# A new written order for the attention and Mish feed-forward kernel: first batch, weight steps and repeating part each at new places

## The chip, the cores and the metric

The kernel runs as one program on one core of a Trainium2 chip. The metric is the device time of one execution in microseconds (us), as the median of three runs. The engines are named as in the profile: PE is TensorE, DVE is VectorE, ACT is ScalarE, POOL is GpSimd and SP is SyncE, which issues most of the transfers.

## What is computed

Cut to what matters (B = 4 batches, H = 8 heads, S = 768 positions, D = 64; d_model = 512, d_ff = 2048):

```
q_assign = argmax(q_n @ c_n.T);  k_assign = argmax(k_n @ c_n.T)   # 16 clusters per head
scores = where(q_assign == k_assign, q @ k.T / 8, -1e9)
attn = softmax(scores) @ v
x = attn with its heads side by side                               # 3072 x 512
h = x @ w_in                                                       # 512 -> 2048
out = (h * tanh(softplus(h))) @ w_out                              # 2048 -> 512
```

## The kernel before

The attention is cut into 32 heads (`n`) of three units each, 96 units (`i`), 24 to a batch. A unit is 256 queries of one head, in two halves (`a`) of 128. One half goes through `scores` (L630 and L635: four matmuls into one of two PSUM buffers of the tag S), `rowmax` (L647, DVE), `expo` (L659, ACT, output `p`), the sum's reciprocal, and a transposition of `p`. In batch 0 PE transposes `p` in f32 (`p_lo`, L707) and DVE and ACT copy the result out of PSUM (L726, L728); in the later batches POOL and DVE split `p` into two f16 parts (`hl`, L697 and L714), and SP transposes these by DMA (L730). `pv` (L750) multiplies by the values for two units at a time into one buffer `o`; in batch 0 a few matmuls more (L762) bring the reciprocals into `o`, and `rb` (L794), `xf` (L795) and two more steps make `x` from it. The two S buffers are shared with the cluster products: `assign_mm` (L542, tile `as`) and `assign_put` (L588, tile `put`) each take one in turn, once for four heads; DVE reads `put` into `stg` (L609), and DMAs carry rows of `stg` into the operands `Z` and `T` of a head (L620, L621). `prep_hi`, `prep_lo` and the four copies make the operands A, B, T and Z of a head, partly on POOL (L483, L486, L499), partly by DMA (L513).

The weights are loaded in 32 steps (`stage`, L240 and L246), rebuilt as f32 (`w_low` L267 on POOL, `w_abs` L258 on ACT, `w_f32` L275 on DVE), squared on PE (`gram`, L295), and scaled into f16 pairs (`w_hi` L333, `w_lo` L346). All of this stands between the units of batch 0.

From unit 24 on the feed-forward network runs beside the attention of the next batch: `m1` (L827 to L829, 12 matmuls of half a tile `h`), `e_mish` (L836), `e_gh` (L840, POOL), `e_gl` (L848, DVE) and `m2` (L864 to L866, six matmuls for each of eight steps `f` of an output tile `O`), then `m_out` (L872). Two `m1` tiles and four `m2` steps go with two units.

No scheduler decides the order. Each operation is entered with a time by `Plan.at`; `Plan.run` sorts them by that number, `after` pulls forward what an operation needs, and `tie` binds the instructions of each engine to that order. The times come from the tables `T` (mostly batch 0) and `N` (the repeating part and, in the lists `u`, `w` and `ws`, one number for each unit and weight step). The numbers are places in a sort, not measured times.

Of the kernel before, what the change touches and what calls it, by code (L numbers as in the profile page):

```python
# [26 lines left out]
class Plan:  # L27
# [9 lines left out]
        self.state = {}  # L37

    def at(self, t, fn, *args):
        self.ops[fn.__name__, *args] = (t, len(self.ops), fn, args)  # L40

    def issue(self, op):
        if op not in self.state:
# [28 lines left out]
def tile_clustered_attention_mish_ffn(  # L72
# [1200 lines left out]
    ('vh', 0): 5,  # L1273
    ('vh', 1): 45,
    'vh_step': 1,
    'v_sqd': -1.793,
    'cent_put': -17.25,
    'ffn': 23.993,
    'w_f': 0.331,
    'w_q': 0.827,  # L1280
    'w_lo': 0.305,
    ('z', 'prep_hi'): -17.4,
    ('z', 'prep_lo'): -15.2,
    ('z', 'copy_t'): -17.3,
    ('z', 'copy_a'): -15.0,
    ('z', 'copy_b'): -15.01,
    ('z', 'copy_z'): -15.1,
    ('z', 'assign_mm'): -15.0,
    ('z', 'assign_turn'): -15.05,
    ('z', 'assign_max'): -14.9,  # L1290
    ('z', 'assign_hot'): -14.8,
    ('z', 'assign_back'): -14.7,
    ('z', 'assign_put'): -14.6,
    ('z', 'hot_direct'): -14.55,
    ('z', 'assign_stg'): -14.4,
    ('z1', 'prep_hi'): -16.637,
    ('z1', 'copy_t'): 0.652,
    ('z1', 'prep_lo'): -0.394,
    ('z1', 'copy_z'): 0.103,
    ('z1', 'copy_b'): 0.753,  # L1300
    ('z1', 'copy_a'): 0.423,
    'as_turn': 1.351,
    'as_max': -0.357,
    'as_hot': 4.283,
    'as_back': 0.815,
    'as_put': 1.374,
    'as_stg': 1.508,
    'n_late': 9,
    'wide': 24,
    'v_s0': 36.614,  # L1310
    'act_q': 3,
    'xbufs': (5, 7, 4),
    'v_sq': 20.406,
    'assign': -1.297,
    'hot_copy': -0.251,
    'copy_a': -0.21,
    'copy_b': -0.38,
    'copy_z': -0.725,
    'copy_t': -0.806,
    'prep_lo': 1.071,  # L1320
    'prep_hi': 3.185,
    'load': -3.206,
    'raw': 4,
    ('f_ws', 0): 0,
    ('f_ws', 1): 1,
# [22 lines left out]
    ('f_b', 1): 1,  # L1348
    ('f_l', 0): 0.096,
    ('f_l', 1): 1,  # L1350
    ('w_l', 0): 2.19,
    ('w_l', 1): 1.226,
    'v0': -19.148,
    'v_d': -1.18,
    ('q_hi', 0): 2.631,
    ('q_lo', 0): 0.521,
    ('q_trans', 0): 0.78,
    ('q_hi', 1): 0.793,
    ('q_lo', 1): 3.324,
    ('q_trans', 1): 1.225,  # L1360
    ('f_w', 0): 1,
    ('f_w', 1): 0.659,
    'units0': 24,
# [5 lines left out]
    'O': 1,  # L1369
    ('ws1', 0): 2.668,  # L1370
    ('ws1', 1): -3.407,
    ('scores', 0): -0.068,
    ('rowmax', 0): -0.01,
    ('expo', 0): 0.345,
    ('recip', 0): 2.622,
    ('scores', 1): 0.349,
    ('rowmax', 1): 0.599,
    ('expo', 1): 6.966,
    ('recip', 1): 1.335,
    'pv': 1.42,  # L1380
    'pv_step': 0.487,
    'v_scale': 0.114,
    'pv_out': 2.609,
    ('w_s', 0): -0.341,
    ('w_s', 1): -0.361,
    ('f_sh', 0): 0.995,
    ('f_sh', 1): 1,
}


N = {
    ('load', 0): -7.458,
    ('load', 1): -10.096,
    ('load', 2): -6.974,
    ('load', 3): -4.979,
    'prep_hi': -3.418,
    'prep_lo': 0.494,
    'copy_t': -2.17,
    'copy_z': -2.427,
    'copy_a': -1.038,  # L1400
    'hot_copy': -2.049,
    'copy_b': -1.075,
    'assign_mm': -4.285,
    'assign_turn': -1.043,
    'assign_max': -4.058,
    'assign_hot': 0.071,
    'assign_back': -3.503,
    'assign_put': -0.183,
    'assign_stg': -2.372,
    'v_load': 16.573,  # L1410
    'v_sq': 18.112,
    'v_scale': 21.77,
    'v_max': 22.2,
    'v_pair': 10,
    'v_high': 26.705,
    'v_low': 27.262,
    'v_d': 2.046,
    'E': [0.355, 0.767, 1.154, 1.513],
    'scores': 2.166,
    'rowmax': -0.272,  # L1420
    'expo': -0.103,
    'total': 6.164,
    'recip': 0.144,
    'p_hi': 11.217,
    'p_lo': 1.549,
    'ptrans': 0.865,
    'pv': [5.55, 13.269, 7.015],
    'pv_out': 6.881,
    'x_lo': 2.789,
    'm1': [0.368, 0.616, 0.939, 1.346],  # L1430
    'e_mish': [4.782, 1.75],
    'e_gh': [1.685, 3.448],
    'e_gl': [1.743, 2.41],
    'm2': [4.854, 4.854, 4.854, 4.854, 4.854, 4.854, 4.854, 4.854, 4.881, 4.881, 4.881, 4.881, 4.881, 4.881, 4.881, 4.881],
    'm_out': -0.431,
    'm_store': 0.376,
# [3 lines left out]
}  # L1440


# [26 lines left out]
```

## Time and profile before

| | us |
|---|---|
| runs of the kernel before | 907.83, 908.76, 910.40 |
| median | 908.76 |
| profiled execution, first to last instruction (span) | 908.0 |
| PE busy in the span | 850.7 (94%) |
| DVE busy | 701.2 (77%) |
| ACT busy | 516.8 (57%) |
| POOL busy | 416.9 (46%) |

The page names the span of the profiled execution and no other time of it; the span stands between the fastest run and the median, 0.76 us under the median. A row of the timeline gives start, length, engine, line, operation and tiles, and in square brackets how long the engine stood idle just before and what ended that. SPq and ACTq are the moments at which an engine's queue issued a DMA.

### The profile page before, as it was taken

To read this page: it belongs to the slowest core of one execution; us is meant where nothing else is said; L and a number is where in the kernel's file an instruction comes from. 1 tells how busy PE (TensorE), PEld (TensorE's weight loads), DVE (VectorE), ACT (ScalarE), POOL (GpSimd) and SP (SyncE) were. 2 spreads that over 40 slices of the span, in tenths; PEclk is the share of its full clock that TensorE was granted. 3 is DMA by queue.
4 is the path that set the end of the run, shared out by engine and by line. 5 is a ranking of instruction groups with operands and counts; after the bars stand their busy time and mean duration, and the time that the engine had idled before them with its cause. 6 is when DMAs were issued, how large, how long until landed. Compare 5 with 4: busy or idle time off the path is not lost.

```text
span 908.0 us, 17381 instructions
## 1 busy us (share of the span) xinstructions
PE 850.7 (94%) x6671; PEld 611.1 (67%) x6671; DVE 701.2 (77%) x1178; ACT 516.8 (57%) x876; POOL 416.9 (46%) x410
## 2 busy tenths in 40 slices
PE   7899788869999999899999999999999999999998
PEld 3666565656667666677667667667667676677787
DVE  7879978777897769788987689699887776378841
ACT  6767867655556565556565666556556565145520
POOL 1443638565556445456555455466555544110000
PEclk9999999999999999999999999999999999999999
DMA  8645582258677796679779787679587675200001
GB/s 326 209 142 161 161 243 59 48 100 170 127 152 156 145 241 117 116 159 182 142 136 173 186 178 144 121 152 197 113 137 150 140 143 93 48 12 12 2 19 41
DMA packets 253058, 121.49 MB, mean 134 GB/s; under 512 B 230288, under 2 KB 230800, under 8 KB 252976
## 3 DMA queue, kind: packets, MB, share of 16 engines
q1 hardware_dynamic: 247632, 108.46, 54.4%
q10 hardware_dynamic: 5344, 11.93, 6.2%
q8 instruction: 52, 0.85, 0.4%
q14 instruction: 30, 0.25, 0.1%
HBM read 35.72 MB, written 6.29 MB: 46 GB/s over the span
## 4 chain that ended last, share of the span: by engine, by line
PE 48%; DVE 22%; issue 9%; ACT 8%; POOL 7%; DMA 5%; ACTq 0%; SPq 0%; POOLq 0%; DVEq 0%
DVE m L647 6%; PE o L750 6%; PE h L827 5%; DVE hl L714 5%; PE h L828 5%; PE h L829 5%; PE s L630 4%; PE O L864 4%; PE O L866 4%; PE O L865 4%; PE s L635 4%; DVE g L848 4%; ACT p L659 3%; POOL g L840 2%; DMA pt<-hl 2%
## 5 line engine op out<-in xcount | busy, mean ns | idle before, releaser
L659 ACT ACTIVATE p<-s,m 128x768 f32<-128x768 f32 x192 | 173.0, 901 | 116.6 <-DVE l L671 89.9
L697 POOL TENSOR_SCALAR hl<-p,l 128x768 f16<-128x768 f32 x144 | 160.2, 1117 | 123.9 <-DVE l L679 43.3
L647 DVE TENSOR_REDUCE m<-s 128x1 f32<-128x768 f32 x192 | 182.4, 950 | 32.2 <-PE s L635 28.8
L714 DVE SCALAR_TENSOR_TENSOR hl<-p,l,hl 128x768 f16<-128x768 f32 x144 | 181.2, 1259 | 8.6 <-POOL hl L697 8.2
L827 PE MATMUL h<-x,w 128*128 128x256 f16 x640 | 176.9, 276 | 3.8 <-ACT u L836 3.6
L828 PE MATMUL h<-x,w 128*128 128x256 f16 x640 | 175.5, 274 | 0.0
L829 PE MATMUL h<-x,w 128*128 128x256 f16 x640 | 175.5, 274 | 0.0
L630 PE MATMUL s<-A,B 128*128 128x384 f32 x384 | 122.0, 399 | 19.9 <-ACT p L659 14.7
L840 POOL TENSOR_SCALAR g<-u,mscg 128x512 f16<-128x512 f32 x80 | 72.5, 906 | 143.6 <-ACT u L836 135.3
L866 PE MATMUL O<-w,g 128*128 128x512 f16 x320 | 121.4, 379 | 7.6 <-DVE g L848 7.6
L864 PE MATMUL O<-w,g 128*128 128x512 f16 x320 | 121.8, 381 | 2.8 <-POOL g L840 2.7
L865 PE MATMUL O<-w,g 128*128 128x512 f16 x320 | 121.3, 379 | 0.0
L635 PE MATMUL s<-Z,T 80*128 80x384 f32 x384 | 100.1, 342 | 0.7 <-DMA T<-stg 0.6
L827 PEld LDWEIGHTS <-w 128*128 128x128 f16 x768 | 75.5, 98 | 32.5 <-issue 21.8
L630 PEld LDWEIGHTS s<-A,B 128*128 128x128 f32 x384 | 62.9, 191 | 44.0 <-ACT p L659 24.3
L848 DVE SCALAR_TENSOR_TENSOR g<-u,mscg,g 128x512 f16<-128x512 f32 x80 | 83.9, 1049 | 9.2 <-POOL g L840 6.8
L659 ACT ACT_TABLE_LOAD x35 | 44.9, 1283 | 79.3 <-DVE m L647 72.1
L828 PEld LDWEIGHTS <-w 128*128 128x128 f16 x768 | 75.9, 99 | 14.9 <-issue 4.2
L829 PEld LDWEIGHTS <-w 128*128 128x128 f16 x768 | 75.5, 98 | 9.0
L750 PE MATMUL o<-pt,v 128*64 128x256 f16 x1296 | 78.1, 274 | 0.5 <-DVE l L671 0.5
L750 PEld LDWEIGHTS <-v 128*64 128x64 f16 x1296 | 67.7, 110 | 15.7 <-issue 12.4
L635 PEld LDWEIGHTS s<-Z,T 80*128 80x128 f32 x384 | 70.2, 190 | 1.5 <-DMA T<-stg 0.9
(225 smaller groups left out, 1311.5 us busy)
## 6 DMA issues: line engine op xcount, KB each, us to landing
qk<-in_qk_dram SPq DMA_DIRECT2D x32, 384.0 KB, 5.0
stage<-in_w_in_dram SPq DMA_DIRECT2D x16, 512.0 KB, 7.6
stage<-in_w_out_dram SPq DMA_DIRECT2D x16, 512.0 KB, 5.1
vraw<-in_vP_dram SPq DMA_DIRECT2D x16, 384.0 KB, 6.5
T<-A ACTq DMA_DIRECT2D x30, 192.0 KB, 3.2
Z<-B SPq DMA_DIRECT2D x30, 192.0 KB, 3.3
B<-T ACTq DMA_DIRECT2D x28, 192.0 KB, 3.7
out_dram<-osb SPq DMA_DIRECT2D x20, 256.0 KB, 4.4
```

The source lines that it names most:

```text
L630: nc.tensor.matmul(s[:, j, :384], st["B", n][:, q0 : q0 + P], st["A", n][:, j * 384 : (j + 1) * 384], start=True, stop=False,)
L635: nc.tensor.matmul(s[:, j, :384], st["T", n][: D + NCL, q0 : q0 + P], st["Z", n][: D + NCL, j * 384 : (j + 1) * 384], start=False, stop=True,)
L647: nc.vector.tensor_reduce(m, st["s", i, a][:, :, :384], axis=AX.XY, op=ALU.max, negate=True)
L659: nc.scalar.activation(p.rearrange("p (n x) -> p n x", n=2), st["s", i, a][:, :, :384], AF.Exp, bias=st["m", i, a], scale=1.0, accum_out=l,)
L697: nc.gpsimd.tensor_scalar(t[:, 0], p, r, 1.0, op0=ALU.mult, op1=ALU.mult)
L714: nc.vector.scalar_tensor_tensor(t[:, 1], p, r, t[:, 0], op0=ALU.mult, op1=ALU.subtract)
L750: nc.tensor.matmul(o[s * D : s * D + D, :256], v if early else v[:, int(part == 1)], st["pt", 2 * m + s][:, :, c + (0 if early or part < 2 ...
L827: nc.tensor.matmul(o, wh, xh, start=(c == 0), stop=False)
L828: nc.tensor.matmul(o, wh, xl, start=False, stop=False)
L829: nc.tensor.matmul(o, wl, xh, start=False, stop=(c == 3))
L864: nc.tensor.matmul(o, gh, wh, start=(f == 0 and fi == 0), stop=False)
L866: nc.tensor.matmul(o, gl, wh, start=False, stop=(f == 7 and fi == 1))
```

## The change

No instruction is added or taken away, and none goes to another engine: each engine has the same instructions as before, in another order. The numbers of the tables are new for the operands of the first heads, all 24 units of batch 0 (`u`), all 32 weight loads (`w`) and 16 scalings (`ws`), and the repeating part; `m2` has one number for each of its 16 steps where there were two values. `Plan.at` gets a table `SHIFT`, which is empty here.

```diff
     def at(self, t, fn, *args):
-        self.ops[fn.__name__, *args] = (t, len(self.ops), fn, args)
+        op = fn.__name__, *args
+        self.ops[op] = (t + SHIFT.get(op, 0), len(self.ops), fn, args)
...
-    ('z', 'hot_direct'): -14.55,
-    ('z', 'assign_stg'): -14.4,
+    ('z', 'hot_direct'): -7.188,
+    ('z', 'assign_stg'): -13.122,
...
-    'm2': [4.854, 4.854, 4.854, 4.854, 4.854, 4.854, 4.854, 4.854, 4.881, 4.881, 4.881, 4.881, 4.881, 4.881, 4.881, 4.881],
+    'm2': [4.92, 5.951, 7.713, 5.196, 5.86, 5.59, 7.546, 4.752, 4.8, 4.886, 6.84, 4.982, 4.196, 4.758, 9.839, 5.211],
...
+SHIFT = {
+   
+}
```

In the order of the change every line number is one higher than before.

**DVE at the start**, from the first cluster product to the maxima of unit 0 (`m0_0` and `m0_1` belong to its two halves). Before:

```order
L573 STREAM_TRANSPOSE hott0_237<-hot0_235 128x768
L600 TENSOR_SCALAR Z_0_200<-put0_239 16x256
L602 TENSOR_SCALAR T_0_192<-put0_239 16x256
L602 TENSOR_SCALAR T_0_192<-putT_243 16x512
L609 TENSOR_SCALAR stg0_253<-put0_239,put_b_137 128x768
L493 SCALAR_TENSOR_TENSOR B_1_270<-qk1_146,scq_138,A_1_196 128x768
L509 CAST Z_1_272<-B_1_270 64x768
L647 TENSOR_REDUCE m0_0_280<-s0_0_275 128x1
```

And now:

```order
L574 STREAM_TRANSPOSE hott0_237<-hot0_235 128x768
L610 TENSOR_SCALAR stg0_249<-put0_239,put_b_137 128x768
L601 TENSOR_SCALAR Z_0_198<-put0_239 16x256
L603 TENSOR_SCALAR T_0_192<-put0_239 16x256
L603 TENSOR_SCALAR T_0_192<-putT_243 16x512
L494 SCALAR_TENSOR_TENSOR B_1_268<-qk1_146,scq_138,A_1_231 128x768
L648 TENSOR_REDUCE m0_0_281<-s0_0_276 128x1
L280 TENSOR_SCALAR w1_284<-w1_284 128x512
```

`stg0` stands first, and the cast `Z_1` has left the rows ahead of `m0_0`. On ACT two of the squares of the values (`vq0_3`, `vq0_2`) stand ahead of `Z_0` now, and the copy `A_1` behind `p0_0`.

**PE and SP around units 9 to 12.** On PE, the product `put1` and its neighbours, before:

```order
L707 MATMUL q8_1_3_983<-ident_129,p8_1_948 128x128 x3
...
L762 MATMUL o3_908<-ident_129,l7_808 64x128 x2
L630 MATMUL s9_1_1000<-A_3_770,B_3_783 128x384 x2
L635 MATMUL s9_1_1000<-Z_3_785,T_3_773 128x384 x2
L588 LDWEIGHTS put_w_136
L588 MATMUL put1_1007<-hott1_962,put_w_136 128x512
```

And now:

```order
L708 MATMUL q8_1_3_978<-ident_129,p8_1_946 128x128 x3
L589 LDWEIGHTS put_w_136
L589 MATMUL put1_984<-hott1_962,put_w_136 128x512
...
L763 MATMUL o3_923<-ident_129,l7_815 64x128 x2
L631 MATMUL s9_1_1005<-A_3_761,B_3_794 128x384 x2
L636 MATMUL s9_1_1005<-Z_3_796,T_3_764 128x384 x2
```

`put1` has moved ahead of the last third of `pv` and of the score `s9_1`. SP's transfers for the operands of head 4, before:

```order
L513 DMA Z_4_1046<-B_4_1044 64x768
L246 DMA stage20_1093<-in_w_out_dram 128x512
L246 DMA stage21_1115<-in_w_out_dram 128x512
L246 DMA stage22_1137<-in_w_out_dram 128x512
L620 DMA Z_4_1046<-stg1_1035 16x768
L621 DMA T_4_1033<-stg1_1035 16x768
L513 DMA A_4_1030<-A_4_1030 64x768
```

And now:

```order
L514 DMA Z_4_1048<-B_4_1046 64x768
L247 DMA stage19_1055<-in_w_out_dram 128x512
L621 DMA Z_4_1048<-stg1_987 16x768
L622 DMA T_4_1021<-stg1_987 16x768
L247 DMA stage21_1136<-in_w_out_dram 128x512
L514 DMA A_4_1018<-A_4_1018 64x768
L247 DMA stage22_1224<-in_w_out_dram 128x512
```

The copies of head 4 have come forward past `stage22`, and two of them past `stage21`.

**DVE in the repeating part**, at unit 42. Before:

```order
L647 TENSOR_REDUCE m42_0_3930<-s42_0_3925 128x1
L714 SCALAR_TENSOR_TENSOR hl41_1_3957<-p41_1_3854,l41_1_3855,hl41_1_3957 128x768
L848 SCALAR_TENSOR_TENSOR g8_3866<-u17_3910,mscg0_2117,g8_3866 128x512
L647 TENSOR_REDUCE m42_1_3968<-s42_1_3963 128x1
L671 TENSOR_SCALAR l42_0_3936<-l42_0_3936 128x1
```

And now:

```order
L648 TENSOR_REDUCE m42_0_3927<-s42_0_3922 128x1
L715 SCALAR_TENSOR_TENSOR hl41_1_3950<-p41_1_3861,l41_1_3862,hl41_1_3950 128x768
L648 TENSOR_REDUCE m42_1_3961<-s42_1_3956 128x1
L672 TENSOR_SCALAR l42_0_3964<-l42_0_3964 128x1
L680 RECIPROCAL l42_0_3964<-l42_0_3964 128x1
```

The split `g8<-u17` has moved from its place ahead of `m42_1` to one behind `m43_1`. On PE, one `m1` half and one `m2` step stood between `s42_0` and `s42_1`; now three `m2` steps stand there, and the 24 matmuls of `m1` follow `s42_1` in one piece. The same holds at units 34, 50, 58, 66, 74, 82 and 90.

## Rows read from the trace of the kernel before

**Rows 1.** Waits of PE by releaser: us in total, times, longest us
```profile
PE s L630 <- ACT p L659: 14.7, 14, 4.3
PE q L707 <- ACT p L659: 10.2, 8, 2.4
PE O L866 <- DVE g L848: 7.6, 15, 0.9
```

**Rows 2.** Windows: us; busy us (instructions) of PE, PEld, DVE, ACT, POOL; clock; DMA
```profile
0.00:200.00 200.00, 165.50 (x1206) 114.27 (x1207) 162.94 (x298) 138.31 (x263) 96.65 (x116) 0.99 0.55 164
200.00:250.00 50.00, 46.90 (x366) 33.16 (x365) 42.17 (x65) 28.50 (x47) 29.15 (x27) 0.94 0.70 136
250.00:800.00 550.00, 534.09 (x4245) 379.86 (x4245) 433.00 (x710) 308.50 (x504) 287.43 (x263) 1.00 0.73 146
```

**Rows 3.** Timeline of the start: DVE, ACT and PE around the first exponential
```profile
18.84 0.56 DVE L509 CAST Z<-B 64x768 fp32r<-64x768 f32 x1
19.31 0.94 DVE L647 TENSOR_REDUCE m<-s 128x1 f32<-128x768 f32 x1
...
19.96 1.21 ACT L258 ACTIVATE w<-stage 128x512 f32<-128x512 f32 x2
21.20 0.90 ACT L659 ACTIVATE p<-s,m 128x768 f32<-128x768 f32 x1
...
22.25 0.87 PE L707 MATMUL q<-ident,p 128*128 128x128 f32 x6 [2.19 <-ACT p L659]
```

**Rows 4.** Timeline of PE and ACT at unit 5
```profile
52.07 0.41 PE L295 MATMUL gram<-w 128*128 128x128 bf16 x4
...
55.30 0.87 PE L707 MATMUL q<-ident,p 128*128 128x128 f32 x6 [1.46 <-ACT p L659]
...
52.18 0.47 ACT L794 ACTIVATE rb<-o,vsp 128x256 f32<-128x256 f32 x1 [0.56 <-PE o L762]
```

**Rows 5.** Timeline of PE and SP's queue at units 10 and 12
```profile
81.14 0.62 PE L630 MATMUL s<-A,B 128*128 128x384 f32 x2 [1.74 <-DVE stg L609]
...
94.31 0.58 PE L630 MATMUL s<-A,B 128*128 128x384 f32 x2 [2.30 <-DMA A<-A]
...
82.18 4.21 SPq L246 DMA_DIRECT2D stage<-in_w_out_dram  x3
...
87.63 0.77 SPq L513 DMA_DIRECT2D A<-A  x1
```

**Rows 6.** Timeline of PE at units 12 and 13
```profile
102.67 0.55 PE L707 MATMUL q<-ident,p 128*128 128x128 f32 x3 [1.24 <-ACT p L659]
...
106.81 0.44 PE L707 MATMUL q<-ident,p 128*128 128x128 f32 x2 [0.77 <-ACT p L659]
...
109.99 0.40 PE L295 MATMUL gram<-w 128*128 128x128 bf16 x4 [1.61 <-DVE w L275]
```

**Rows 7.** Timeline of PE and ACT at units 16 and 22
```profile
129.69 0.55 PE L707 MATMUL q<-ident,p 128*128 128x128 f32 x3 [2.41 <-ACT p L659]
...
161.44 0.62 PE L630 MATMUL s<-A,B 128*128 128x384 f32 x2 [0.81 <-ACT p L659]
...
128.27 0.48 ACT L728 COPY pt<-q 128x384 f32<-128x384 f32 x1 [3.10 <-DMA Z<-B]
```

**Rows 8.** Timeline of PE at the passage from batch 0 to the repeating part
```profile
190.64 0.27 PE L827 MATMUL h<-x,w 128*128 128x256 f16 x1 [3.00 <-ACT u L836]
...
198.43 0.62 PE L630 MATMUL s<-A,B 128*128 128x384 f32 x2 [4.28 <-ACT p L659]
```

**Rows 9.** Window after the wait at 127.3 us (columns as in rows 2)
```profile
130.70:134.10 3.40, 3.40 (x20) 2.13 (x20) 1.99 (x4) 1.89 (x4) 0.00 (x0) 0.50 0.92 276
```

**Rows 10.** Timeline of the repeating part: one m2 step, and a score's maximum on DVE
```profile
453.42 0.38 PE L864 MATMUL O<-w,g 128*128 128x512 f16 x1
...
454.71 0.49 PE L588 MATMUL put<-hott,put_w 128*128 128x512 bf16 x2
...
458.88 0.52 PE L635 MATMUL s<-Z,T 80*128 80x384 f32 x2
...
462.69 0.96 DVE L647 TENSOR_REDUCE m<-s 128x1 f32<-128x768 f32 x1
```

More of the change, by code (lines that the diff above doesn't have):

```diff
@@ L1275 @@
     'vh_step': 1,
-    'v_sqd': -1.793,
-    'cent_put': -17.25,
+    'v_sqd': -4.857,
+    'cent_put': -17.279,
     'ffn': 23.993,
[L1279 to L1293, printed above, removed]
-    ('z', 'hot_direct'): -14.55,
-    ('z', 'assign_stg'): -14.4,
[L1296 to L1307, printed above, removed]
+    'w_f': 0.342,
+    'w_q': 0.823,
+    'w_lo': 0.291,
+    ('z', 'prep_hi'): -18.102,
+    ('z', 'prep_lo'): -12.511,
+    ('z', 'copy_t'): -17.558,
+    ('z', 'copy_a'): -14.141,
+    ('z', 'copy_b'): -14.199,
+    ('z', 'copy_z'): -16.644,
+    ('z', 'assign_mm'): -11.201,
+    ('z', 'assign_turn'): -12.664,
+    ('z', 'assign_max'): -16.42,
+    ('z', 'assign_hot'): -13.075,
+    ('z', 'assign_back'): -13.196,
+    ('z', 'assign_put'): -12.749,
+    ('z', 'hot_direct'): -7.188,
+    ('z', 'assign_stg'): -13.122,
+    ('z1', 'prep_hi'): -15.657,
+    ('z1', 'copy_t'): -0.271,
+    ('z1', 'prep_lo'): -1.37,
+    ('z1', 'copy_z'): 1.133,
+    ('z1', 'copy_b'): 2.654,
+    ('z1', 'copy_a'): 0.617,
+    'as_turn': 1.904,
+    'as_max': -0.501,
+    'as_hot': 2.44,
+    'as_back': 0.862,
+    'as_put': 0.993,
+    'as_stg': 1.052,
     'n_late': 9,
     'wide': 24,
-    'v_s0': 36.614,
+    'v_s0': 37.618,
     'act_q': 3,
     'xbufs': (5, 7, 4),
[L1313 to L1322, printed above, removed]
+    'v_sq': 20.251,
+    'assign': -1.302,
+    'hot_copy': -0.44,
+    'copy_a': -0.208,
+    'copy_b': -0.408,
+    'copy_z': -0.704,
+    'copy_t': -0.829,
+    'prep_lo': 0.861,
+    'prep_hi': 1.193,
+    'load': -4.609,
     'raw': 4,
@@ L1350 @@
     ('f_l', 1): 1,
[L1351 to L1360, printed above, removed]
+    ('w_l', 0): 1.964,
+    ('w_l', 1): 0.963,
+    'v0': -17.969,
+    'v_d': -4.561,
+    ('q_hi', 0): 2.074,
+    ('q_lo', 0): 0.677,
+    ('q_trans', 0): 0.738,
+    ('q_hi', 1): 0.779,
+    ('q_lo', 1): 4.003,
+    ('q_trans', 1): 1.217,
     ('f_w', 0): 1,
@@ L1371 @@
     ('ws1', 1): -3.407,
[L1372 to L1376, printed above, removed]
+    ('scores', 0): -0.15,
+    ('rowmax', 0): 0.017,
+    ('expo', 0): 0.325,
+    ('recip', 0): 3.718,
+    ('scores', 1): 0.365,
     ('rowmax', 1): 0.599,
-    ('expo', 1): 6.966,
-    ('recip', 1): 1.335,
+    ('expo', 1): 3.444,
+    ('recip', 1): 1.374,
     'pv': 1.42,
-    'pv_step': 0.487,
+    'pv_step': 0.48,
     'v_scale': 0.114,
-    'pv_out': 2.609,
-    ('w_s', 0): -0.341,
-    ('w_s', 1): -0.361,
+    'pv_out': 2.591,
+    ('w_s', 0): 0.201,
+    ('w_s', 1): 0.013,
     ('f_sh', 0): 0.995,
@@ L1391 @@
 N = {
[L1392 to L1411, printed above, removed]
+    ('load', 0): -8.996,
+    ('load', 1): -9.577,
+    ('load', 2): -6.846,
+    ('load', 3): -5.647,
+    'prep_hi': -3.463,
+    'prep_lo': 1.938,
+    'copy_t': -2.608,
+    'copy_z': -2.367,
+    'copy_a': -1.572,
+    'hot_copy': -1.879,
+    'copy_b': -1.003,
+    'assign_mm': -4.289,
+    'assign_turn': -3.32,
+    'assign_max': -4.063,
+    'assign_hot': 1.158,
+    'assign_back': -3.461,
+    'assign_put': 0.705,
+    'assign_stg': -2.445,
+    'v_load': 17.332,
+    'v_sq': 18.055,
     'v_scale': 21.77,
-    'v_max': 22.2,
+    'v_max': 20.003,
     'v_pair': 10,
[L1415 to L1419, printed above, removed]
-    'rowmax': -0.272,
[L1421 to L1433, printed above, removed]
-    'm2': [4.854, 4.854, 4.854, 4.854, 4.854, 4.854, 4.854, 4.854, 4.881, 4.881, 4.881, 4.881, 4.881, 4.881, 4.881, 4.881],
-    'm_out': -0.431,
-    'm_store': 0.376,
[3 rows of a table removed]
+    'v_high': 26.688,
+    'v_low': 27.388,
+    'v_d': 2.039,
+    'E': [0.374, 0.767, 1.238, 1.512],
+    'scores': 1.455,
+    'rowmax': -0.272,
+    'expo': 1.674,
+    'total': 10.193,
+    'recip': 0.131,
+    'p_hi': 11.909,
+    'p_lo': 2.229,
+    'ptrans': 0.846,
+    'pv': [5.141, 16.228, 4.578],
+    'pv_out': 8.203,
+    'x_lo': 2.802,
+    'm1': [0.536, 0.632, 1.227, 1.52],
+    'e_mish': [6.518, 1.693],
+    'e_gh': [1.692, 2.151],
+    'e_gl': [1.771, 3.432],
+    'm2': [4.92, 5.951, 7.713, 5.196, 5.86, 5.59, 7.546, 4.752, 4.8, 4.886, 6.84, 4.982, 4.196, 4.758, 9.839, 5.211],
+    'm_out': -0.434,
+    'm_store': 0.3,
[3 rows of a table added]
+}
+SHIFT = {
 }
```

6 rows, old and new, of the table N are left out of this document.

## The prediction

> **What bounds the kernel now.** I read the busy shares first, then PE's busy time by stretches, then PE's waits by releaser, and last the timeline around each long wait. By stretches [rows 2] PE is the bound of the repeating part: of the 550 us from 250 to 800 it is busy for 534.09, so all that an order could win there is 15.9 us. The first 200 us are different. PE is busy for 165.50 of them and idle for 34.5, while DVE is busy for 162.94: no engine is full, and the end is set by chains that go from one engine to the next. The waits by releaser [rows 1] say which chains: 14.7 us of scores and 10.2 us of transpositions that wait for an exponential on ACT. Only the third, 7.6 us in 15 short waits of the second layer for DVE's `g`, lies in the repeating part. As the change moves instructions and changes none, its effect is the sum of waits that it ends and of waits that it makes.
>
> **The change part by part.** I went through PE's long waits of the first 200 us and asked for each what stands in the new order between its cause and its end.
>
> (a) *Start.* The first transposition waits 2.19 us for the first exponential `p0_0`, which started at 21.20, right behind two weight conversions that ran from 19.96 to 21.17 [rows 3]. Its maximum had been there since 20.25, and 0.56 us of that was the cast `Z_1` ahead of it. Now the squares of the values stand in a gap of ACT before the first cluster product, the copy `A_1` stands behind `p0_0`, and `Z_1` behind `m0_0`. With `stg0` first, the second score no longer waits for its buffer either. I see `p0_0` some 2 us earlier; of that 0.2 is lost again at unit 2. Term: 1.8, bounds 0 and 2.19.
>
> (b) *Unit 5.* Between the end of `rb`'s source (its ACT step starts at 52.18) and the transposition at 55.30 runs a chain rb, xf, x, copy, exponential; PE had one piece of `gram` of 0.41 us to put there, and waited 1.46 [rows 4]. Now four such pieces stand there, three more than before, which covers 1.2 us. Term: 1.1, bounds 0 and 1.46.
>
> (c) *Unit 10.* The score waited 1.74 us until DVE had read `put1` out of one of the two score buffers [rows 5]. `put1` stands now ahead of a third of `pv` and of a whole score, and DVE reads it ahead of `xf` and of a maximum. Term: 1.7, bounds 0 and 1.74.
>
> (d) *Unit 12.* The score waited 2.30 us for the landing of `A<-A`. SP had issued that copy at 87.63, held up by three weight loads, whose issue took from 82.18 to 86.39 since each waits for a stage buffer [rows 5]. Now the copy stands ahead of `stage22`, with only `stage19` and `stage21` between it and `Z_4`, and two stage buffers are freed sooner on DVE. It should be issued some 4 us sooner, more than the wait. Term: 2.3, bounds 0 and 2.30; what it moves back, `stage22`, is a weight step of which no multiplication is near.
>
> (e) *Units 12 and 13.* Three waits, 1.24, 0.77 and 1.61 us [rows 6]. In each, one weight conversion that stood ahead of the awaited operation on ACT or POOL stands behind it now, or the `o` tile that DVE's queue waits for is finished one score earlier. One conversion is 0.6 us [rows 3]. Term: 3 x 0.6 = 1.8, bounds 0 and 3.62.
>
> (f) *Unit 16.* PE waited 2.41 us; ACT had stood for 3.10 us, until `B_6` could be issued after the landing of `Z_6` [rows 7]. The order on ACT is the same there. What changed is what is under way beside `Z_6`: the four value loads stand farther behind it, one weight load is issued after it and no longer before it. The trace has no row for `Z_6` without this company, so the bounds are 0 and 2.41; I take the middle, 1.2, since a reason speaks for each end.
>
> (g) *Unit 22.* 0.81 us behind `put2` [rows 7]; a whole transposition of 0.87 us (length as in rows 3) stands now between the score whose buffer is awaited and the waiting one. Term 0.8.
>
> (h) *Passage.* Waits of 3.00 and 4.28 us [rows 8]. The second ends a chain of mish, POOL's and DVE's split, a maximum, a table load and an exponential; its order on DVE is the same, so that it stays. In the first, PE has 24 matmuls and two scores to place where it had fewer, but the mish comes about 1 us later, behind one more exponential. Term: 0.8, bounds -1 and 3.
>
> The sum is 1.8 + 1.1 + 1.7 + 2.3 + 1.8 + 1.2 + 0.8 + 0.8 = 11.5 us. I count 60% of it, 6.9 us. The reason is the next thing that is late: five of the eight waits are for an exponential, whose maximum stands in DVE's queue, and without 11.5 us of span DVE would be busy for 163 of 188 us, 87%. The repeating part shows DVE at 433.00 of 550, 79%, with PE full [rows 2], so that a part of what PE stops waiting for will be DVE's lateness instead.
>
> In the *repeating part* I cost the change at nothing. The `m2` steps now stand together behind `pv`; that gives DVE's `g` time and takes the same time from the score that follows. At the eight units where `g` moved behind the next maximum the second exponential comes sooner; at two of the cluster products the next score comes closer behind and will wait up to 1 us. Work that hides the rest: PE itself, full for 97% of that stretch. What it costs if that cover goes is the second rival.
>
> The profiled execution has a span of 908.0 us. 908.0 - 6.9 = 901.1, and with the 0.76 us by which the median stands above it, **901.9**.
>
> [...]
>
> **The rivals.** *Given back (0.20).* The eight waits go, and the exponential or the buffer that was next in line holds PE instead: at six of the eight places the awaited operation has only one operation of 0.5 to 1 us less ahead of it. For it: DVE and PE are about equally busy in the first 200 us [rows 2]. Against it: (c), (d) and (g) are single late events, no chains. Time: 40% of 6.9 counted, about 906 to 910, say 908.
>
> *DVE held in the repeating part (0.13), slower.* At eight units three `m2` steps now stand between the two scores of a unit, and DVE has the second maximum right behind one split, with the `g` that could fill the gap behind it. An `m2` step takes 454.71 - 453.42 = 1.29 us [rows 10], so the second score ends about 3 x 1.29 + 0.9 = 4.8 us after the first. DVE fills 0.96 of this with the first maximum and some 1.2 with the split and then stands, up to 2.6 us at each of eight places, 21 us in all, and everything in its queue is late by that. The point from which it decides is DVE's own lateness: if its first maximum starts over 2.6 us after its score, it never stands. In the row the score ended at 459.40 and the maximum started at 462.69, 3.3 us later [rows 10], which speaks against it; at other units DVE waits for scores. With two thirds of the price and the gain of batch 0: 908.76 - 6.9 + 14 = 916.
>
> [...]
>
> *The repeating part gains too (0.11).* The 15 waits for `g` [rows 1] go, and so does a third of the 15.9 us of idle time; batch 0 gives all of its 11.5: 908.76 - 11.5 - 5.3 = 892.
>
> *The change does nothing* is ruled out for the order, which differs on every engine; the new table `SHIFT` adds 0 to every number.
>
> **How the numbers follow.** The forecast has 0.56, with 6.9 us of 11.5 and room from 3 to 11.5: 897 to 906. A measurement of this kernel can tell about 0.3%, 2.7 us, from no change: under 906.0 is faster, over 911.5 slower. Faster: 0.56 + 0.11 = 0.67; within 0.3%: 0.20; slower: 0.13. The range reaches from 893, which takes in most of the last rival and the upper bounds of the terms, to 911, the end of *given back*; it leaves out the slower case and a little below.
>
> **What would show it.** Right: PE busy in the first 200 us over 170 (165.50 before); no wait for `stg`, none for the DMA `A<-A`; the first transposition before 20.8 us; PE's waits for exponentials under 20 us in all (24.9); from 250 to 800 an equal amount of PE work in 547 to 553 us. Wrong: waits of PE for exponentials that grow behind units 34, 42, 50 and so on, with DVE idle between two maxima (the slower rival), or the same idle time of PE in batch 0 under other releasers (given back).

## The result, and the profile after

The change is **faster by more than was forecast, and outside the range**: median 886.54 us (882.48 to 886.74, 4 runs) against 909.18 us (907.83 to 910.40, 4 runs). The ratio is 0.9735 (95% interval 0.9707 to 0.9762), some 24 us where 7 were forecast. A second set of runs, `after_again` below, gave 0.975 (0.9731 to 0.977). One of the 12 runs of `m2_old` below took 3025.89 us; its ratio leaves that run out.

The profiled execution has a span of 884.7 us and took 886.58 us. So the time lies 1.9 us above the span; my working took the span of before as if it were 0.8 us under the median, which made the forecast about 1 us too low. That is small beside the rest.

Part 1 of the page of the changed kernel, the span and the busy times:

```profile
span 884.7 us, 17422 instructions
...
PE 846.5 (96%) x6670; PEld 616.9 (70%) x6671; DVE 681.6 (77%) x1178; ACT 513.6 (58%) x876; POOL 414.4 (47%) x410
```

The busy times hardly moved except DVE's, which was 701.2 us: the same instructions take 20 us less there. More on that at the end. (The page of before counts 17381 instructions. The 41 more are not work of the engines: 42 more semaphore instructions of their queues, and one matmul's record less.)

To compare stages I cut the changed kernel where PE has done as many instructions as before at 200, 250 and 800 us [rows 2]: 1206, then 366 more, then 4245 more (to two instructions). Windows of the changed kernel (columns as in rows 2):

```profile
0.00:193.50 193.50, 166.04 (x1206) 116.07 (x1208) 161.94 (x299) 138.43 (x264) 97.07 (x117) 0.97 0.57 168
193.50:242.60 49.10, 45.98 (x368) 33.47 (x365) 42.23 (x67) 28.61 (x46) 28.63 (x27) 0.96 0.82 152
242.60:777.50 534.90, 530.94 (x4247) 384.00 (x4246) 414.02 (x708) 305.09 (x502) 284.35 (x264) 1.00 0.79 149
777.50:884.70 107.20, 103.58 (x855) 83.39 (x853) 63.44 (x107) 41.48 (x64) 4.35 (x5) 0.99 0.05 16
```

The first stage takes 6.5 us less, the passage 0.9, **the repeating part 15.1**, the tail 0.8. In the repeating part PE's idle time fell from 15.9 to 4.0 us. (The two orders interleave the same work a little differently, so that a stage is good to 2 us or so.) One order also differs from execution to execution: cut in the same way, the second profile of the change, after_again, has 190.3, 49.55 and 537.65 us. Between the two profiles the first stage thus gains 6.5 to 9.7 us and the repeating part 12.4 to 15.1.

PE's waits by releaser in the changed kernel (line, releaser: us in total, times, longest us):

```profile
PE s L631 <- ACT p L660: 9.5, 8, 4.2
PE q L708 <- ACT p L660: 8.3, 11, 1.4
PE gram L296 <- DVE w L276: 4.6, 4, 1.9
PE o L751 <- DMA pt<-hl: 4.2, 3, 1.8
PE s L319 <- DVE ws1m L314: 1.8, 1, 1.8
...
PE s L631 <- DVE stg L610: 0.7, 1, 0.7
...
PE O L867 <- DVE g L849: 0.4, 1, 0.4
```

Beside rows 1: the waits for exponentials went from 24.9 to 17.8 us, those of the second layer for `g` from 7.6 to 0.4, and those for POOL's half of `g`, 2.7 us before, are gone. New are 4.2 us for the transposed splits `pt`, and waits of `gram` for the weights grew from 2.0 to 4.6. Taking all waits of PE over 0.25 us: up to 180 us 25.9 us before and 20.1 now; in the passage (180 to 240 us) 9.9 and 9.2; after it 15.3 and 4.0. In the repeating part alone PE's waits were these before (250 to 800 us) and are these now (242.6 to 777.5 us):

```profile
PE O L866 <- DVE g L848: 7.2, 14, 0.9
PE s L630 <- ACT p L659: 5.4, 8, 1.5
PE O L864 <- POOL g L840: 2.7, 4, 0.8
```

```profile
PE o L751 <- DMA pt<-hl: 2.9, 2, 1.8
PE s L631 <- ACT p L660: 0.7, 2, 0.4
PE O L867 <- DVE g L849: 0.4, 1, 0.4
```

### The profile page after: what moved, and what is told of

The parts are those of the page before. It is cut to its first block, busy times and chain, and to the rows that moved or that the text cites. A ratio compares the mean times of both kernels' runs of the same rounds, so it can differ in the third digit from the quotient of the medians.

```text
span 884.7 us, 17422 instructions
## 1 busy us (share of the span) xinstructions
PE 846.5 (96%) x6670; PEld 616.9 (70%) x6671; DVE 681.6 (77%) x1178; ACT 513.6 (58%) x876; POOL 414.4 (47%) x410
## 4 chain that ended last, share of the span: by engine, by line
PE 70%; DVE 12%; ACT 7%; issue 4%; DMA 4%; POOL 2%; ACTq 0%; SPq 0%; DVEq 0%; POOLq 0%
PE o L751 8%; PE h L828 8%; PE h L829 8%; PE h L830 8%; PE O L865 7%; PE O L867 7%; PE O L866 7%; PE s L631 6%; PE s L636 5%; DVE m L648 4%; ACT p L660 2%; DMA pt<-hl 2%; DVE hl L715 2%; PE q L708 1%; ACT L660 1%
## 5 line engine op out<-in xcount | busy, mean ns | idle before, releaser
L698 POOL TENSOR_SCALAR hl<-p,l 128x768 f16<-128x768 f32 x144 | 155.3, 1081 | 94.2 <-DVE l L680 50.8
L715 DVE SCALAR_TENSOR_TENSOR hl<-p,l,hl 128x768 f16<-128x768 f32 x144 | 167.3, 1162 | 3.5 <-POOL hl L698 3.2
L841 POOL TENSOR_SCALAR g<-u,mscg 128x512 f16<-128x512 f32 x80 | 67.8, 851 | 158.4 <-ACT u L837 151.2
L849 DVE SCALAR_TENSOR_TENSOR g<-u,mscg,g 128x512 f16<-128x512 f32 x80 | 72.6, 908 | 7.2 <-POOL g L841 6.6
```

The source lines that it names most:

```text
L715: nc.vector.scalar_tensor_tensor(t[:, 1], p, r, t[:, 0], op0=ALU.mult, op1=ALU.subtract)
```

## The experiments

But for the entries in `SHIFT` of the last part, each kernel swaps groups of numbers between the tables of before and of the change; the instructions are always the same. Every ratio is against the kernel of before on the same chip. "Repeating part" in a table is the time for the 4247 PE instructions that follow the first 1574, from windows cut as above.

### The change in halves

`first_new` has the new numbers of batch 0 and the weights alone; `rep_new` the others alone. `ffn_new` has only the second layer's new numbers, `att_new` only the attention's in the repeating part. One line of each edit against before:

```diff
# first_new: tables T, and u, w, ws of N
-    'as_put': 1.374,
+    'as_put': 0.993,
# ffn_new: m1, e_mish, e_gh, e_gl, m2, m_out, m_store
-    'e_gl': [1.743, 2.41],
+    'e_gl': [1.771, 3.432],
# att_new: everything else in N but u, w, ws
-    'scores': 2.166,
+    'scores': 1.455,
# rep_new: ffn_new and att_new together
```

> The numbers of batch 0 and of the weights are new, those of the repeating part and of the second layer are as before. Theory A (the two parts gain apart from each other, and batch 0 gave about what was counted for it): at equal amounts of PE work the change was 5.8 us ahead at 207 us of before's span and 8.6 us at 238 us, so 7 us less than before, about 902, with PE's waits for DVE's g back at 7 to 8 us. Rival B (batch 0 hands its operands over earlier and that is what frees the repeating part): under 892.

> The numbers of the repeating part and of the second layer are new, those of batch 0 and of the weights are as before. Theory A: the other 15 us, about 894, with PE's waits for DVE's g under 1 us. Rival B: over 903. A third case, an overlap of the two (the repeating part can only run as far ahead as PE is full): the two gains of this and of the kernel with a new batch 0 add up to clearly more than 22.6 us.

> Only the second layer's numbers are new (m1, e_mish, e_gh, e_gl, m2, m_out, m_store). Theory F (what PE no longer waits for is g, which m2 now meets later): 10.3 us of waits of m2 for DVE's and POOL's g go, so 897 to 901. Rival G (attention and second layer interleave, and one half of the numbers without the other puts instructions at unmeant places): no gain or slower, 908 to 925.

> Only the attention's numbers in the repeating part are new (operands, cluster products, values, E, scores to pv), second layer as before. Theory F: only the waits of scores for exponentials gain, some 3 to 5 us, 904 to 906, and the waits for g stay at 7 us or more. Rival G: no gain or slower, 908 to 925.

| | median us | ratio (95%) | repeating part, us | second layer's waits for `g` (DVE, POOL), us |
|---|---|---|---|---|
| before | 908.24 | 1 | 550.0 | 7.6, 2.7 |
| first_new | 903.01 | 0.994 (0.9927 to 0.9953) | 548.9 | 7.6, 2.7 |
| rep_new | 901.69 | 0.9915 (0.9888 to 0.9943) | 535.7 | 0.6, 0 |
| ffn_new | 901.64 | 0.9923 (0.9904 to 0.9942) | 541.6 | 1.9, 0 |
| att_new | 925.97 | 1.0184 (1.0157 to 1.0212) | 559.0 | 7.2, 6.4 |

Windows of first_new, of rep_new and of att_new:

```profile
0.00:195.30 195.30, 167.16 (x1206) 116.65 (x1207) 162.27 (x298) 138.44 (x264) 97.45 (x116) 0.95 0.58 168
...
244.60:793.50 548.90, 534.19 (x4247) 379.56 (x4246) 432.48 (x710) 308.27 (x504) 288.08 (x264) 1.00 0.73 146
```

```profile
0.00:202.10 202.10, 169.53 (x1206) 118.49 (x1207) 163.24 (x297) 139.00 (x264) 94.45 (x116) 0.96 0.54 160
...
249.65:785.30 535.65, 531.71 (x4247) 383.84 (x4246) 413.24 (x707) 305.06 (x502) 285.34 (x264) 1.00 0.79 149
```

```profile
257.75:816.70 558.95, 535.44 (x4247) 382.55 (x4246) 434.46 (x709) 307.48 (x504) 290.97 (x264) 1.00 0.74 143
```

Theory A holds for first_new: batch 0 gives 5.5 us, close to the 6.9 that I had counted, and its repeating part is that of before. It holds for the repeating part of rep_new too, 14.3 us less with the old batch 0, and rival B, which wanted over 903, missed as well. But the time of rep_new is not theory A's, which said about 894: the median is 901.69, and its six runs went from 895.4 to 905.6 us, the profiled one being the fastest. By the medians the two parts do **not** add up: 5.5 and 7.7 us (10 in `rep_again` below) against some 24 for both, so that 8 to 11 us of the gain come only where both are new. In ffn_new most of the waits for `g` go, 10.3 us to 1.9, as theory F said, though the time stayed 0.6 us above its range. Att_new was rival G's: the attention's new numbers, without the second layer's, **cost** 9 us in the repeating part and 17 in all. The two sets belong together.

### m2 alone, and everything but m2

```diff
# m2_old, from the change; m2_new is the kernel of before with the same line the other way
-    'm2': [4.92, 5.951, 7.713, 5.196, 5.86, 5.59, 7.546, 4.752, 4.8, 4.886, 6.84, 4.982, 4.196, 4.758, 9.839, 5.211],
+    'm2': [4.854, 4.854, 4.854, 4.854, 4.854, 4.854, 4.854, 4.854, 4.881, 4.881, 4.881, 4.881, 4.881, 4.881, 4.881, 4.881],
```

> The changed kernel with the two old values for m2 in place of the 16 new ones, all else as changed. Theory M (what ends PE's waits in the repeating part is that m2 stands later, so that g is there): the waits of m2 for DVE's and POOL's g come back from 0.4 us to 7 us or more, and the time to 894 to 900. Theory D (DVE makes g sooner, since it has 25 us less to do where fewer of its splits run beside POOL): waits for g stay under 3 us and the time within 3 us of 886.5.

> The kernel of before with the 16 new numbers of m2 alone. Theory M: the waits for g fall from 10.3 us (DVE's and POOL's) to under 3 us, time 900 to 903, as with all numbers of the second layer. Theory D: DVE's order is as before and its g as late, so waits for g stay at 7 us or more, 906 to 910.

m2_old: 907.74 us, ratio 0.9971 (0.995 to 0.9993). **One line of the table takes back nearly the whole gain**; its repeating part is 559.05 us. Its largest wait of PE, by releaser, and the wait for `g`:

```profile
PE O L867 <- DVE l L672: 14.3, 9, 2.0
...
PE O L867 <- DVE g L849: 8.8, 8, 1.2
```

The `l` named first is a neighbour of `g`, as the timeline shows, first DVE's, then PE's row of the wait:

```profile
359.31 1.15 DVE L849 SCALAR_TENSOR_TENSOR g<-u,mscg,g 128x512 f16<-128x512 f32 x1
360.38 0.14 DVE L672 TENSOR_SCALAR l<-l 128x1 f32<-128x1 f32 x1
```

```profile
360.52 0.39 PE L867 MATMUL O<-w,g 128*128 128x512 f16 x1 [1.67 <-DVE l L672]
```

`g` ends at 359.31 + 1.15 = 360.46, and PE goes on at 360.52. It is the same at all nine of these waits: `g` ends 57 to 59 ns before PE goes on, as at the eight that are named after it. So both rows are waits for `g`, 23.1 us in all, where before had 10.3: the other new numbers put `g` later (the second `e_gl` went from 2.41 to 3.432), and only the later `m2` makes that free. Theory M, with twice the price it had set. Theory D falls with it, since DVE's splits `hl` and `g` are as short in m2_old as in the change (1171 and 856 ns on average against 1162 and 908).

m2_new: 914.10 us, ratio 1.0048 (1.0031 to 1.0066). Here theory M missed. The waits for `g` fell nearly as it said, to 3.4 us (2.1 and, for POOL's half, 1.3), but the time rose. Waits of m2_new by releaser:

```profile
PE s L631 <- ACT p L660: 16.8, 16, 4.3
PE q L708 <- ACT p L660: 10.5, 9, 2.2
PE h L828 <- ACT u L837: 5.6, 4, 3.0
...
PE O L867 <- DVE g L849: 2.1, 6, 0.5
```

Against rows 1 and 8, 5.5 us of waits for DVE's `g` became 2.4 us of waits for exponentials and 2.0 of waits for mish (3.6 before), and the repeating part takes 550.30 us as before. The later `m2` is **needed but not enough**: moved alone, it hands the time that `g` gets to the scores and to mish.

### The attention's share

Starting from the change and putting back the attention's old numbers shows what they add to the second layer's.

```diff
# att_old: all of the attention's numbers of the repeating part; att_old_load: all but the loads
-    'scores': 1.455,
+    'scores': 2.166,
# att_old alone
-    ('load', 0): -8.996,
+    ('load', 0): -7.458,
# ffn_load: ffn_new with the new numbers of 'load'
```

> The kernel of before with the new numbers of the second layer and the new ones of the q/k loads. With the second layer's alone, PE's cluster products waited for the load of q and k (their 45 inner steps of the middle 400 us took 165 ns from start to start in place of 75, some 4 us). Theory L (the new loads, 1 to 1.5 units sooner, are what the second layer's numbers lack): these steps are back at 75 ns, and the time is 3 to 5 us under that of the second layer's numbers alone, 897 to 898.5. Rival: the load is late for another reason (its buffer is free no sooner), no difference: 900 to 903.

> The changed kernel with the attention's old numbers in the repeating part; batch 0, weights and second layer as changed. Theory L (the new attention numbers serve the second layer's new places, above all by sooner loads of q and k): between equal amounts of PE work in the steady part it lost 5.3 us where the second layer alone was new, so 890 to 895, with the 45 inner steps of the cluster products of the middle 400 us back at about 165 ns. Rival (by the medians of the kernels with an old batch 0, 901.6 and 899.9 to 901.7, the attention's numbers bring nothing once the second layer's are there): 885 to 888.

> As the kernel before it, but with the new numbers of the q/k loads. Theory L: the inner steps of the cluster products are at 75 ns, and 4 us of the loss are back, 886 to 891. Rival: within 1 us of the kernel before it.

| | median us | ratio (95%) |
|---|---|---|
| ffn_load (ffn_new: 901.64, 0.9923) | 901.25 | 0.9905 (0.9878 to 0.9932) |
| att_old | 896.99 | 0.9861 (0.9844 to 0.9879) |
| att_old_load | 893.02 | 0.9822 (0.9802 to 0.9841) |

Between att_old and att_old_load, on one chip, lie 4.0 us, as theory L said, though both times came out 2 us above its ranges, and the 45 steps from one matmul of a cluster product to the next went from 156 to 75 ns, which is 3.7 us. That the 4.0 us come through these steps is not shown: the profiled repeating part took 541.40 us in att_old and 543.10 in att_old_load, where PE waited 3.11 us for `pt` at 329.7 us and the mean clock was 0.99. In ffn_load the time did not follow: the passage took 52.8 us (50.8 in ffn_new), and PE waited 2.4 us for `pt` at 337 us. So the sooner loads pay with the new batch 0; with the old one no gain can be told.

Of the last part, two more kernels tell the score chain from the operands:

```diff
# score_old: E, scores, rowmax, expo, total, recip, p_hi, p_lo, ptrans, pv, pv_out, x_lo
-    'p_lo': 2.229,
+    'p_lo': 1.549,
# ops_old: prep_*, copy_*, hot_copy, assign_*
-    'assign_turn': -3.32,
+    'assign_turn': -1.043,
```

> The changed kernel once more, on the same chip as the three beside it. 884 to 888, ratio 0.971 to 0.977.

> The changed kernel with the old numbers of E and of the score chain (scores, rowmax, expo, total, recip, p_hi, p_lo, ptrans, pv, pv_out, x_lo) in the repeating part. What of the attention's numbers gave the last 6 to 8 us is still open. Theory S (the score chain: where its splits stand against g on DVE and POOL): this kernel loses 5 us or more, 890 to 896. Rival O (the operands and cluster products): it stays within 2 us of the changed kernel beside it.

> The changed kernel with the old numbers of the operands (prep, copies) and of the cluster products in the repeating part; the loads of q and k and the score chain as changed. Theory S: within 2 us of the changed kernel beside it. Rival O: 5 us or more slower, 890 to 896.

The changed kernel beside them: 886.21 us (0.975). score_old: 891.68 us, 0.9811 (0.979 to 0.9831), 5.5 us more. The time is theory S's, its reason is not shown: in the repeating part of score_old PE waits for no `g`, but 4.1 us for exponentials (0.7 in the change), and DVE is busy for 422.96 us (414.02 in the change). ops_old: 883.61 us, 0.9719 (0.9699 to 0.974); the operands' new numbers bring nothing, if anything they cost. The same kernel once more:

> The changed kernel with the old operands and cluster products once more. If it is truly under the changed kernel (0.9719 against 0.975 of before), its ratio to before lies again under 0.9735: 881 to 885. If that was chance of one chip: 885 to 888.

It gave 886.48 us, 0.9744 (0.9719 to 0.9769): no difference from the change that can be told.

So the gain can be counted up as a ladder, by ratios to before and with 909 us: batch 0 5.5 us; the second layer on top of it 7.2 (0.994 to 0.9861); the loads 3.5 (to 0.9822); the rest of the attention, most of it the score chain, 6.5 to 7.9 (to 0.975 and 0.9735). Each step is a difference of two ratios whose intervals are 0.003 to 0.006 wide, and it holds for this order of steps only: the second layer's numbers alone, ffn_new, gave 7.0 us without the new batch 0, the attention's alone cost 17.

### The spread of rep_new, and the start

> The kernel with the new repeating part and the old batch 0 once more, for the spread of its runs (895.4 to 905.6). Theory H (the spread is PE at half clock around the passage to the repeating part, which starts where PE is full): time goes with the mean granted clock, about 9 us for 0.010 of it, and a run of 900 or more shows more microseconds at a clock of 0.50 than the 16 us or so of the one at 895.4. Rival: the spread comes with waits in the repeating part; then from 350 to 750 us PE is busy for under 394 us (396.06 in the run at 895.4).

rep_again ran in 899.12 to 901.17 us (median 899.88, ratio 0.9888, 0.9862 to 0.9913) at clocks of 0.987 to 0.992, in no order of the clock: theory H fell as far as the passage goes. (Its rival fell too: PE is busy for 395.06 us from 350 to 750.) But the profile shows a stretch at half clock where the theory had none, in the second 20 us. The window from 20 to 40 us of before, of rep_again, of start_old (next) and of the change:

```profile
20.00:40.00 20.00, 15.26 (x121) 11.41 (x120) 16.07 (x31) 15.28 (x31) 8.46 (x12) 1.00 0.54 176
```

```profile
20.00:40.00 20.00, 16.75 (x96) 13.38 (x95) 13.44 (x28) 14.27 (x30) 4.91 (x9) 0.74 0.48 157
```

```profile
20.00:40.00 20.00, 16.85 (x121) 13.11 (x120) 16.30 (x34) 15.85 (x32) 8.06 (x11) 0.91 0.68 224
```

```profile
20.00:40.00 20.00, 18.06 (x145) 13.93 (x146) 19.03 (x39) 17.15 (x35) 10.28 (x15) 1.00 0.83 273
```

With the granted clock of 0.50 in rows 9, a mean of 0.74 comes to about half of these 20 us at 0.50, by my estimate. Of the eight profiled kernels with the old start, seven have a mean clock of 0.74 or 0.91 here, and before has 1.00; all twelve with the new start have 1.00. The one profile that I predicted from was the exception. What is it worth?

```diff
# start_old: the changed kernel with the old ('z', ...), ('z1', ...), v_sq, v_sqd, v0, cent_put and units 0 and 1
-    ('z', 'assign_stg'): -13.122,
+    ('z', 'assign_stg'): -14.4,
```

> The changed kernel with the old numbers for the operands of the first two heads, the first cluster product, the values' squares and units 0 and 1. Theory H (the long wait for the first exponential is followed, in most executions, by PE at half clock between 20 and 40 us: a granted clock of 0.74 to 0.91 there in six of seven profiled kernels with the old batch 0, 1.00 in all three with the new one): that stretch has a clock under 0.95 and the kernel loses the 1.0 to 2.2 us of the wait and up to 3 us to the clock, 888.5 to 892. Rival: the start's order is worth its wait alone and the clock stays at 1.00, 887 to 888.5.

start_old: 887.65 us, 0.9773 (0.9748 to 0.9797). The clock was as theory H said, 0.91, and PE was 24 matmuls behind in that window; the time is in the rival's range. It is 1.1 and 1.4 us above the two medians of the change, 2.1 to 3.5 by the ratios, and the intervals overlap, so that what the start's order is worth is **not settled**. Nor do the profiles settle it. PE's 1206th instruction ends at 194.0 us in start_old and at 193.7 in the change, as if the loss had been made up; but that execution of the change ran at a mean clock of 0.57 from 128 to 136 us, and in after_again, with 1.00 there, the same instruction ends at 190.5.

Why rep_new and rep_again, with the whole old batch 0, stay 13 to 15 us above the change, when the new batch 0 is worth 5.5 us to the kernel of before, is left open. The profiles show where the difference lies: in rep_again the passage (49.2 us) and the repeating part (536.7) are like those of the change, and the difference is in the first stage. PE's 1206th instruction ends there at 198.4 to 206.9 us in the seven profiles with the whole old batch 0 (200.3 in before, 205.1 in rep_again) and at 189.8 to 195.6 in the nine with the whole new one and no entry in `SHIFT`. So what batch 0 is worth changes from execution to execution and with the repeating part beside it, and the profile that I predicted from is one of the faster ones of its order.

### The passage

Of the two waits of the passage [rows 8] the first, 3.00 us for mish, fell to 1.03 (at 184.25 us). The second, 4.28 us, did not go: in the changed kernel a score still waits 4.16 us. DVE, ACT and PE there:

```profile
185.02 1.38 DVE L849 SCALAR_TENSOR_TENSOR g<-u,mscg,g 128x512 f16<-128x512 f32 x1 [0.58 <-POOL g L841]
...
186.33 1.44 DVE L715 SCALAR_TENSOR_TENSOR hl<-p,l,hl 128x768 f16<-128x768 f32 x1
...
187.80 0.96 DVE L648 TENSOR_REDUCE m<-s 128x1 f32<-128x768 f32 x1
...
188.86 1.28 ACT L660 ACT_TABLE_LOAD   x1 [4.08 <-DVE m L648]
...
191.20 1.01 PE L631 MATMUL s<-A,B 128*128 128x384 f32 x2 [4.16 <-ACT p L660]
```

The maximum at 187.80 had its score since 181.4, where PE's last matmul of it ends; two splits stand ahead of it on DVE, which I took to be needed much later. Two kernels move them, with entries in `SHIFT`:

```diff
# pass: at units 26 and 28 both maxima ahead of g and of hl
+    ('e_gl', 0): 0.732,
+    ('ptrans', 25, 0): 0.414,
+    ('ptrans', 25, 1): 0.142,
...
# pass2: each maximum ahead of the hl before it, g behind them all
+    ('rowmax', 26, 0): -0.02,
+    ('rowmax', 26, 1): -0.14,
+    ('e_gl', 0): 0.611,
+    ('e_gh', 0): 0.685,
...
```

On POOL, pass also puts a `g` ahead of one `hl` at each of the two places, and pass2 both `hl` ahead of both `g`; the orders of PE and ACT are those of the change in both.

> The changed kernel with six entries in SHIFT: on DVE, at units 26 and 28, both maxima stand ahead of the split g and of the two splits hl of the unit before, in place of behind the first two and the third of these; PE's order is the same. Theory P (PE's waits of 4.16 and 1.80 us at the passage are for an exponential whose maximum stood in DVE's queue behind splits that nobody needed for 10 us): both waits fall under 1 us, and the clock of 0.50 behind the first one goes or shrinks, 878 to 883. Rival (given back: the transposed splits come later and PE's second product with the values waits for them): the wait for pt at about 214 us grows from 1.3 to 4 us or more, 885 to 888.

> The passage again: at units 26 and 28 each maximum stands ahead of the split hl that stood before it, and the second layer's split g, on DVE and POOL, behind all four. With the maxima alone first, PE's waits for exponentials went and it waited 3.82 and 3.41 us for the transposed splits in their place. Theory P2 (the splits can be sooner as well, since only g has time): the waits for pt at the two places fall under 1.5 us each and the time is 3 us or more under the changed kernel beside it, 880 to 884. Rival (the chain exponential, split, transposition, landing is what bounds the passage, in whatever order): the two places still cost PE 4 us or more, and the time is within 1.5 us of the changed kernel.

> The two pieces that came out under the changed kernel in one: old operands and cluster products, and the passage with splits and maxima ahead of g. If the two gains (2.6 and 1.1 us) are of different places they add: 1 us under the kernel beside it or more, 880 to 883. If the passage's gain is given back in the transposed splits, which wait for SP's queue here as there: within 1 us of the kernel beside it, or over it.

pass: 885.77 us, 0.9741 (0.9724 to 0.9759). pass2: 885.07 us, 0.9736 (0.9708 to 0.9764), beside 886.21 for the change. ops_pass: 886.03 us, 0.9744 (0.9719 to 0.9769). None can be told from the change. PE's rows in pass, the score that had waited and the product with the values that follows, then the same product in pass2:

```profile
185.34 0.44 PE L631 MATMUL s<-A,B 128*128 128x384 f32 x1 [0.83 <-ACT p L660]
```

```profile
193.71 0.52 PE L751 MATMUL o<-pt,v 128*64 128x256 f16 x6 [3.82 <-DMA pt<-hl]
```

```profile
192.43 0.84 PE L751 MATMUL o<-pt,v 128*64 128x256 f16 x11 [0.93 <-DMA pt<-hl]
195.60 0.61 PE L751 MATMUL o<-pt,v 128*64 128x256 f16 x6 [2.33 <-DVE v L430]
```

Theory P ended the waits that it named, though the mean clock from 180 to 230 us stayed at 0.93, and its rival took the gain back: `pv` waits for the transposed splits instead, 3.82 us here and 3.41 at 210.95 us. As POOL's half of a split stands behind a `g` in pass, that wait may be POOL's doing as well as DVE's. In pass2, with the splits sooner on both, `pv` waits for the values' split `v`, and at 210.78 us 2.28 us for `pt`: 5.5 us at the two places, as the rival of pass2 said. In these two orders a wait that is ended comes back at the next link of the chain.

## Why the prediction was wrong

**The step that failed** is this one: "In the *repeating part* I cost the change at nothing." It gave 15.1 us in one profile and 12.4 in the other. The reason behind it was that the later `m2` "gives DVE's `g` time and takes the same time from the score that follows". The first half came true: PE's waits for `g` there fell from 9.9 us (7.2 and, for POOL's half, 2.7) to 0.4. The second half, for which I had no row, did not: the waits of scores for exponentials fell too, from 5.4 us to 0.7, and only 2.9 us for `pt` are new. For `m2` moved alone it would have been right: m2_new keeps its 550 us there, with 6.7 us of waits for exponentials and 2.0 for mish. The other new numbers lift it. The cover that I named, "PE itself, full for 97% of that stretch", was no reason: 15.9 us were idle there, I had written so in the first paragraph, and the change took 12 of them, and 3 more of PE's busy time, of which no run shows the source. The price stood under a rival (0.11) and was too low there also, 5.3 us from a third of the idle time.

**The slower rival**, DVE held between two maxima, did not occur. DVE around unit 42 in the changed kernel:

```profile
315.19 0.96 DVE L648 TENSOR_REDUCE m<-s 128x1 f32<-128x768 f32 x1
316.07 2.38 DVE L715 SCALAR_TENSOR_TENSOR hl<-p,l,hl 128x768 f16<-128x768 f32 x1
318.38 0.94 DVE L648 TENSOR_REDUCE m<-s 128x1 f32<-128x768 f32 x1
```

No idle time stands in front of the second maximum; at units 34, 50 and 58 it is 0.35, 0 and 0.16 us, where I had allowed 2.6. DVE runs behind PE there, as rows 10 had said.

**Batch 0** came out near its sum: 6.9 counted, 6.5 and 9.7 in the windows of the two profiles, 5.5 in first_new. That waits went and others took part of their place is what the cut to 60% was for, but the hit is partly luck: (a) gave 1.0 or 0.5 us in place of 1.8, behind the 2.30 of (d) stand two new waits of 1.41, and what DVE was late with was less the maxima that I had named than the weights (`gram` and `ws1m` wait 6.4 us for them, 2.7 before). By terms:

| | forecast | in the changed kernel |
|---|---|---|
| (a) start | 2.19 less 1.8 | 1.19 remains, first transposition at 20.95 (22.25 before); 1.66 and 21.50 in after_again |
| (b) unit 5 | 1.46 less 1.1 | 0.85 remains |
| (c) unit 10 | 1.74 gone | gone; `gram` waits 1.47 for a weight at 76.87 |
| (d) unit 12 | 2.30 gone | gone; two waits of 1.41 for exponentials at 89.93 and 97.25 |
| (e) units 12, 13 | 3.62 less 1.8 | 1.90 at 104.04, again `gram` for a weight |
| (f) unit 16 | 2.41 less 1.2 | 0.44; but 1.84 for `ws1m` at 129.58 (0.68 before) |
| (g) unit 22 | 0.81 less 0.8 | 0.68, now for `stg` of `put2` |
| (h) passage | 9.5 with the third wait of 2.24, less 0.8 | 9.2 in five waits |

Of the signs: PE busy in the first 200 us over 170 (it is 172.5), no wait for `A<-A`, waits for exponentials under 20 us (17.8) came true; "no wait for `stg`" and the start before 20.8 us just missed; equal work from 250 to 800 in 547 to 553 us was wrong, 535.

*The clock behind (f).* Behind the wait of 2.41 us stood a stretch at a granted clock of 0.50 [rows 9]. The wait went to 0.44, but in this execution such a stretch comes with the wait of 1.84 us: the clock is 0.50 from 129.1 to 135.8 us, and the mean from 128 to 136 us is 0.57. Nine profiles have this wait, of 1.84 to 1.86 us, at 127 to 130 us. The mean clock of these 8 us is 0.57 to 0.79 in five of them (the change, ops_old, score_old, pass, pass2) and 1.00 in four (after_again, m2_old, ops_again, ops_pass). So the same wait comes with half clock in some executions and without it in others, and what halves the clock is not shown.

## What to carry to other kernels

A bound at 97% of a stretch still leaves what the other 3% are worth, here most of a gain of 12 to 15 us of 908: divide them by releaser and ask of each what the change does to it, before a term is set to nothing. In a written order a consumer's place and its producers' places are one decision: later `m2` alone cost 4 us, the rest without it gained 3, both together gained 24 (0.9735), so this order had to be judged whole, and its halves did not sum. A wait that was ended at the passage was worth only what the next link of the same chain allowed; run such a move before counting it.

## What the runs showed that I had not expected

**DVE's and POOL's splits take longer side by side.** The same 144 splits `hl` and 80 `g` took 181.2 + 83.9 = 265.1 us on DVE before and 167.3 + 72.6 = 239.9 after. One split beside POOL and then one alone, from the kernel of before, DVE's rows and then POOL's:

```profile
452.37 2.56 DVE L714 SCALAR_TENSOR_TENSOR hl<-p,l,hl 128x768 f16<-128x768 f32 x1
...
457.81 1.01 DVE L714 SCALAR_TENSOR_TENSOR hl<-p,l,hl 128x768 f16<-128x768 f32 x1
```

```profile
451.43 0.91 POOL L697 TENSOR_SCALAR hl<-p,l 128x768 f16<-128x768 f32 x1 [2.37 <-issue]
452.30 1.81 POOL L499 TENSOR_TENSOR B<-qk,A 128x768 fp32r<-128x768 f32 x1
454.09 1.61 POOL L697 TENSOR_SCALAR hl<-p,l 128x768 f16<-128x768 f32 x1
```

Beside POOL's `B` the split takes 2.56 us, and ends 0.82 us after `B`; the one at unit 42 above, 2.38 us, does so too (POOL's `B` runs there from 315.82 for 1.81 us). In all 26 pairs of the two profiles in which the split starts while `B` runs, it ends 0.81 or 0.82 us after `B`, where a whole split alone takes 1.01. POOL's own half, behind `B` and beside DVE's, takes 1.61 us, and 0.91 ahead of it. Of the 144, 60 had under 0.2 us of a POOL instruction beside them before, and each of those took 0.998 to 1.019 us, the other 84 on average 1.43; now 74 took 1.001 to 1.019, the other 70 on average 1.32. What makes the two engines slower side by side is not shown.

The shorter splits are not enough for the gain: m2_old has them as well, and not the time. That they are no part of it is **not shown**. DVE is busy for 432 to 437 us of the repeating part in the four kernels in which that part takes 548.9 us or more (before, first_new, att_new, m2_new), and for 413 to 423 in all those in which it takes 543.1 or less; m2_old, with 410 us and waits for `g`, is the one exception. No kernel changes the splits' company and nothing else.

**Half clock in seven of eight executions with the old start.** They had a mean clock of 0.74 or 0.91 in their second 20 us, by my estimate some 4 to 10 us at the clock of 0.50 of rows 9; the eighth, the kernel of before, had 1.00. What this costs in the end is open, as start_old shows.
